# Moving the second half of an SBUF copy from ScalarE to VectorE in an attention and mixture-of-experts kernel

## Chip, cores and metric

The kernel runs on one core of one Trainium2 chip. The metric is the device time of one execution in microseconds (us); lower is better.

## What is computed

Three stages follow each other. First a chunked attention over 4 batches, 8 heads, 768 positions and a head size of 64: a chunk of 32 queries sees its own 32 keys, 16 to the left, 8 to the right and 8 memory keys. Then a soft mixture of experts, and then a top-2 mixture of experts, both over 3072 rows of 512 columns, with 8 experts of hidden size 1024. Cut to its core the reference is:

```python
for c in range(nc):                                   # 24 chunks of 32 queries
    k_full = concat([mem_k, k[:, :, l_start:r_end]])  # 8 + up to 56 keys
    v_full = concat([mem_v, v[:, :, l_start:r_end]])
    a = softmax(scale * q_c @ k_full.T)
    out[:, :, c_start:c_end] = a @ v_full
x = out.transpose(0, 2, 1, 3).reshape(3072, 512)
logits = x @ phi                                      # soft experts: 8 experts, 4 slots each
slot_input = softmax(logits, axis=0).T @ x
slot_out[e] = relu(slot_input[e] @ w1[e]) @ w2[e]
x = softmax(logits, axis=1) @ slot_out
top2 = the two largest of x @ w_gate + log1p(exp(x @ w_noise)) * noise
out[n] = sum over top2 of weight * (relu(x[n] @ w1[e]) @ w2[e])
```

## The kernel before

**Order of the work.** The program is written in the order in which each engine executes it (a manual schedule). Each engine runs its own instructions in that order and waits only for the semaphores that its next instruction needs. All large transfers are issued by SyncE in one queue; the small loads of `mem_v` are issued by GpSimd.

**The attention stage** (function `attention`, about the first 160 us) works through 32 items, numbered `i`. An item is one pair of heads of one batch and one half of the sequence (12 chunks); a pair of items shares one `q` and one `k` load. One pass of the main loop (a round here) makes these steps, each on the engine named:

- `qk(i+1)`: TensorE multiplies queries and keys into a PSUM tile `st` (lines 1062 and 1069).
- `mxr(i+1)` and `sub(i+1)`: VectorE clears the corner of `st`, takes the row maximum and subtracts it into `a` (lines 1077 to 1088).
- `tr(i+3)`: TensorE transposes a raw `q` or `k` tile, ScalarE copies it out of PSUM in four pieces (lines 1043 and 1050), and SyncE loads the raw tile three further on (line 996).
- `spread(i+1, 0)` and `spread(i+1, 1)`: copies of `v`, below.
- `expo(i+1)`: ScalarE takes the exponential (line 1092).
- `at(i)`, `atc(i)`: TensorE transposes the probabilities, ScalarE copies them out of PSUM into `aT` (lines 1097 and 1103).
- `av(i-1)`, `nrm(i-1)`: TensorE multiplies with `v` (line 1112), VectorE divides by the row sum into `xs` (lines 1121 to 1124). Behind them SyncE and GpSimd load the `v` of item `i+3` into the buffer that `av(i-1)` has just read (`load_v`, lines 1013 and 1022).
- `xt(i-2)`, `xtc(i-2)`: TensorE transposes `xs`, VectorE copies it into `xT` (lines 1135 and 1142). Six times in the stage `lg`, `lgc`, `lt` and `ltc` turn `xT` into logits (ScalarE line 1156, VectorE line 1166).
- In every second round SyncE issues a piece of 512 KB of the weights of the soft experts (`load_piece`, line 148).

The last four rounds are not in the loop; their steps stand in the table `ORDER`, mixed with the first softmax of the soft experts.

**The copies of `v`.** Four tiles `VB` in rotation hold the `v` of an item. Rows 0 to 63 belong to the first head of the pair and rows 64 to 127 to the second. Head `h` is loaded by one transfer of SyncE (28 rows of each chunk) and one of GpSimd (4 rows of `mem_v`). A loaded row holds two positions next to each other (128 columns), and one half of them has to stand on 32 other partitions for the product. `spread(i, h)` makes that copy, 32 partitions by 12 chunks by 64 columns, float32, SBUF to SBUF. It waits for the two transfers of its head, and `av(i)` waits for it:

```python
    def spread(i, h):
        ...
        if h:
            nc.scalar.activation(o, x, AF.Copy)       # second head: ScalarE, line 1031
        else:
            nc.vector.tensor_copy(o, x)               # first head: VectorE, line 1033
```

In the loop `spread(n, 0)` stands ahead of `sub(n)`, and `spread(n, 1)` behind `atc(i)` and ahead of `av(i-1)` and `nrm(i-1)`.

**After the attention.** From about 150 us on SyncE issues the weights of the remaining soft experts (line 148: into the arena that held `v`, `k` and the raw tiles, into `xs` and into two weight tiles), and then those of the first expert of the top-2 stage (line 200). TensorE computes the soft experts as the weights land (function `soft`, lines 238 to 258). The top-2 stage begins with its gate at about 230 us and ends with the kernel.

Of the kernel before, what the change touches and what calls it, by code (L numbers as in the profile page):

```python
# [13 lines left out]
AF = mybir.ActivationFunctionType  # L14
# [949 lines left out]
def attention(tc, nc, q, k, v, mem_k, mem_v, phi, xs, L, K, phis, arena, ab, wk, ps, load_piece):  # L964
# [35 lines left out]
    def vcols(i, p, n, col, cols, c0=0, c1=NH):  # L1000
        return custom(VB[i % NV][p:p + n], c0 * VC + col, [[VC, c1 - c0], [1, cols]])
# [25 lines left out]
    def spread(i, h):  # L1027
        o, x = (vcols(i, 32, 32, 64, D), vcols(i, 0, 32, 0, D)) if h == 0 else \
            (vcols(i, 96, 32, 130, D), vcols(i, 64, 32, VC, D))
        if h:  # L1030
            nc.scalar.activation(o, x, AF.Copy)  # L1031
        else:
            nc.vector.tensor_copy(o, x)  # L1033

    def tr(n):
        u, x = divmod(n, 2)
# [258 lines left out]
    nc.gpsimd.memset(one, 1.0)  # L1295
    load_v(3)
    spread(0, 0)
    spread(0, 1)
    qk(0)
    mxr(0)  # L1300
# [4 lines left out]
    for i in range(I0):  # L1305
# [5 lines left out]
        if i == 6:  # L1311
            nc.gpsimd.dma_start(phis, phi.rearrange("(j p) s -> p j s", p=128))
        spread(n, 0)
        sub(n)
        expo(n)
# [51 lines left out]
```

## Time and profile before

| | |
|---|---|
| median of 3 runs | 600.06 us (598.2 to 609.83) |
| the profiled execution: its time | 601.2 us |
| its span, first to last instruction | 599.4 us |
| mean granted clock of TensorE | 0.936 of full speed |
| busy: TensorE (PE) | 498.9 us, 83% |
| busy: VectorE (DVE) | 332.0 us, 55% |
| busy: ScalarE (ACT) | 291.6 us, 49% |
| busy: GpSimd (POOL) | 290.3 us, 48% |
| moved by DMA | 127.35 MB, mean 212 GB/s |

PE, DVE, ACT, POOL and SP are TensorE, VectorE, ScalarE, GpSimd and SyncE; PEld is TensorE's weight load, and SPq is SyncE issuing a transfer. L1033 is line 1033 of the kernel. A row names the line, the engine, the operation and the tiles as out<-in with partitions x elements, then xcount. "Idle before" is the idle time of the engine just ahead of the instruction, and the arrow says what ended it. The DMA share is the mean busy share of the 16 DMA engines; overlapping packets can carry it a little over 1.

### The profile page before, as it was taken

The page shows a single profiled execution, that of the slowest core. Times are in us where ns is not written, and L with a number is a line of the kernel's source. Part 1 is how long each engine was busy: PE and PEld are TensorE (multiplying, and loading weights), DVE is VectorE, ACT ScalarE, POOL GpSimd, SP SyncE. Part 2 cuts the span into 40 slices and gives each one's busy share as a digit, 9 for nine tenths or more (in the row PEclk, how much of TensorE's full clock was granted, in tenths as well). Part 3 has the DMA queues.
Part 4 walks back from the last instruction along what each step waited for, and adds up shares of the span by engine and source line. Part 5 has one row for each costly group of instructions (what it writes and reads, how often), then busy time and mean ns, then how long its engine had stood idle before and what let it go on. Part 6 is the DMA issues. An engine that isn't in the chain of part 4 may idle for free.

```text
span 599.4 us, 15297 instructions
## 1 busy us (share of the span) xinstructions
PE 498.9 (83%) x5437; PEld 274.1 (46%) x5437; DVE 332.0 (55%) x827; ACT 291.6 (49%) x510; POOL 290.3 (48%) x260
## 2 busy tenths in 40 slices
PE   5776988869889677365989899999999999989960
PEld 4655766647543124232534445545545455435520
DVE  6565767657863004898565755748566465622200
ACT  5876989868521104753532715526354263533210
POOL 6132322222012000693566765758576577877662
PEclk9998999999999867597989989999999999989995
DMA  9999999999999998959388696887869876436552
GB/s 206 231 217 213 241 240 262 229 221 241 315 412 362 412 415 241 349 179 254 52 248 226 111 265 152 233 226 170 224 150 264 215 183 119 80 69 111 75 63 26
DMA packets 99509, 127.35 MB, mean 212 GB/s; under 512 B 19238, under 2 KB 68026, under 8 KB 99434
## 3 DMA queue, kind: packets, MB, share of 16 engines
q1 hardware_dynamic: 79866, 109.30, 60.7%
q0 software_dynamic: 19152, 16.89, 21.2%
q8 instruction: 49, 0.80, 0.6%
q14 instruction: 26, 0.21, 0.1%
q10 hardware_dynamic: 416, 0.15, 0.1%
HBM read 94.84 MB, written 20.42 MB: 192 GB/s over the span
## 4 chain that ended last, share of the span: by engine, by line
PE 37%; DVE 7%; DMA 5%; issue 4%; POOL 3%; ACT 2%; SPq 0%; POOLq 0%; DVEq 0%; ACTq 0%
PE l L739 30%; DMA out_dram<-y,idx 4%; PE l L705 3%; POOL out_dram L770 2%; PE g L362 2%; DVE W L428 1%; DMA C<-G 1%; DVE W L544 1%; PE l L736 1%; DVE lo L715 1%; POOL cg L664 1%; ACT W L424 1%; DVE G L411 1%; DVE W L812 1%; ACT hi L707 0%
## 5 line engine op out<-in xcount | busy, mean ns | idle before, releaser
L770 POOL DMA_INDIRECT out_dram<-y,idx x96 | 155.8, 1622 | 83.3 <-DMA out_dram<-y,idx 40.7
L739 PE MATMUL l<-W,hi 128*128 (+1 forms) x768 | 182.5, 392 | 1.2 <-DVE W L428 0.8
L715 DVE SCALAR_TENSOR_TENSOR lo<-l,hi 128x1024 f16<-128x1024 f32 x49 | 59.9, 1222 | 112.3 <-ACT hi L707 97.8
L739 PEld LDWEIGHTS <-hi 128*128 128x128 f16 x768 | 75.2, 100 | 88.9 <-issue 14.3
L757 ACT ACTIVATE y<-l,gw 128x512 f32<-128x512 f32 x49 | 33.5, 684 | 156.1 <-PE l L739 94.0
L739 PE MATMUL l<-W,lo 128*128 (+1 forms) x384 | 90.8, 379 | 4.6 <-DVE lo L715 4.6
L1022 POOL DMA_DIRECT2D arena<-in_mem_v_dram x64 | 39.3, 615 | 105.1 <-PE av L1112 105.1
L664 POOL DMA_INDIRECT cg<-table,idx x49 | 51.1, 1044 | 20.4 <-issue 10.5
L739 PEld LDWEIGHTS <-lo 128*128 128x128 f16 x384 | 36.9, 98 | 48.5 <-DVE lo L715 5.2
L707 ACT ACTIVATE hi<-l 128x1024 f16<-128x1024 f32 x49 | 50.2, 1024 | 10.3 <-PE l L705 10.2
L1069 PE MATMUL st<-arena,qT 128*32 128x112 f32 (+2 forms) x768 | 31.8, 271 | 16.2 <-ACT arena L1050 9.9
L428 DVE SCALAR_TENSOR_TENSOR W<-w,sc,W 128x1024 f16<-128x1024 f32 x31 | 42.3, 1390 | 0.2
L1050 ACT ACTIVATE qT<-tr 64x384 f32<-64x384 f32 x64 | 33.2, 518 | 9.3 <-PE tr L1043 8.2
L1033 DVE COPY arena<-arena 32x768 f32<-32x768 f32 x32 | 17.8, 556 | 35.2 <-DMA arena<-in_v_dram 30.6
L1043 PE MATMUL tr<-cf,arena 128*128 128x128 f32 x192 | 31.2, 304 | 6.2 <-DMA arena<-in_q_dram 5.4
L424 ACT ACTIVATE W<-w,sc 128x1024 f16<-128x1024 f32 x32 | 35.7, 1149 | 0.2
L1112 PE MATMUL av<-arena,aT 128*32 128x130 f32 x768 | 29.3, 283 | 4.2 <-issue 3.5
L1050 ACT ACTIVATE arena<-tr 64x384 f32<-64x384 f32 x64 | 30.9, 484 | 2.3 <-PE tr L1043 1.6
L374 DVE TENSOR_REDUCE mxp<-w 128x1 f32<-128x2048 f32 x13 | 29.6, 2275 | 0.0
L1043 PEld LDWEIGHTS tr<-cf,arena 128*128 128x128 f32 x192 | 22.9, 153 | 13.8 <-issue 6.7
L1062 PE MATMUL st<-arena,qT 128*32 128x16 f32 x768 | 25.7, 188 | 2.8 <-issue 2.8
L1031 ACT ACTIVATE arena<-arena 32x768 f32<-32x768 f32 x32 | 26.9, 842 | 1.6 <-issue 0.7
(268 smaller groups left out, 680.3 us busy)
## 6 DMA issues: line engine op xcount, KB each, us to landing
w<-in_moe_w_dram SPq DMA_DIRECT2D x88, 512.0 KB
arena<-in_moe_w_dram SPq DMA_DIRECT2D x28, 512.0 KB
arena<-in_v_dram SPq DMA_DIRECT2D x62, 168.0 KB
arena<-in_q_dram SPq DMA_DIRECT2D x16, 384.0 KB
arena<-in_k_dram SPq DMA_DIRECT2D x16, 384.0 KB
xs<-in_moe_w_dram SPq DMA_DIRECT2D x12, 512.0 KB
out_dram<-zt SPq DMA_DIRECT2D x14, 384.0 KB
C<-G SPq DMA_DIRECT2D x21, 256.0 KB
```

What stands on the lines that cost most here:

```text
L424: nc.scalar.activation(hi, w2, AF.Copy, scale=sc[:, rk, 5:6])
L428: stt(lo, w2, sc[:, rk, 5:6], hi, op0=OP.mult, op1=OP.subtract)
L664: nc.gpsimd.indirect_dma_start(out=CG[i], out_offset=None, in_=table, in_offset=bass.IndirectOffsetOnAxis(ap=idx[:, i:i + 1], axis=0))
L707: nc.scalar.activation(HI[i], p, AF.Relu)
L715: stt(LO[i].rearrange("p k t -> p (k t)"), p.rearrange("p k t -> p (k t)"), 0.0, HI[i].rearrange("p k t -> p (k t)"), op0=OP.max, op1=OP.s ...
L739: nc.tensor.matmul(P2[i], h[i][:, k, :], dyn(W2f, i, w * 4096 + 512 * k, 512, RG.get(i)), start=x == 0 and k == 0, stop=x == last and k == 7)
L757: nc.scalar.activation(YV[i], P2.pop(i), AF.Copy, scale=GW.pop(i))
L770: nc.gpsimd.indirect_dma_start(out=o, out_offset=bass.IndirectOffsetOnAxis(ap=idx[:, i:i + 1], axis=0), in_=y[:, DH * h:DH * h + DH], in_o ...
L1022: nc.gpsimd.dma_start(vcols(i, p + 28, 4, col, 128), bass.AP(tensor=mem_v.tensor, offset=mem_v.offset + (b * H + 2 * hp + h) * NMEM * D, a ...
L1043: nc.tensor.transpose(p[:, T, :], src[:, h, T, :], identf)
L1050: nc.scalar.activation(o, i, AF.Copy)
L1069: nc.tensor.matmul(st[32 * j:32 * j + 32, g, :, w0:w1], QT[u][:, 32 * c:32 * c + 32], kb[:, :, 16 * c + w0:16 * c + w1], start=True, stop= ...
```

## The change

Both halves of the copy are made by VectorE; nothing else is edited.

```diff
     def spread(i, h):
         o, x = (vcols(i, 32, 32, 64, D), vcols(i, 0, 32, 0, D)) if h == 0 else \
             (vcols(i, 96, 32, 130, D), vcols(i, 64, 32, VC, D))
-        if h:
-            nc.scalar.activation(o, x, AF.Copy)
-        else:
-            nc.vector.tensor_copy(o, x)
+        nc.vector.tensor_copy(o, x)
```

The lines behind it stand three lines higher in the changed kernel: 1050 is 1047 there, 1033 is 1030, and so on. Names as `xT_89` and `xT_90` are the two tiles `xT`.

ScalarE, one round of the loop and the start of the next, before:

```order
L1050 ACTIVATE arena<-tr 64x384 x4
L1092 ACTIVATE a<-a 128x384
L1103 ACTIVATE aT<-at 128x384
L1031 ACTIVATE arena<-arena 32x12x64
L1050 ACTIVATE qT<-tr 64x384 x4
```

and with the change:

```order
L1047 ACTIVATE arena<-tr 64x384 x4
L1089 ACTIVATE a<-a 128x384
L1100 ACTIVATE aT<-at 128x384
L1047 ACTIVATE qT<-tr 64x384 x4
L1089 ACTIVATE a<-a 128x384
```

The copy `arena<-arena` is gone, and the four copies of the next transpose (`<-tr`) follow `aT<-at` at once.

VectorE, one round of the loop, before:

```order
L1079 MEMSET st 32x4x4
L1082 TENSOR_REDUCE mx<-st 128x6
L1033 COPY arena<-arena 32x12x64
L1088 TENSOR_TENSOR a<-st,mx 128x384
L1121 TENSOR_SCALAR rc<-av 128x6
L1122 RECIPROCAL rc<-rc 128x6
L1124 TENSOR_TENSOR xs<-av,rc 128x3x128
L1142 COPY xT_89<-xt 128x384
```

and with the change:

```order
L1076 MEMSET st 32x4x4
L1079 TENSOR_REDUCE mx<-st 128x6
L1030 COPY arena<-arena 32x12x64
L1085 TENSOR_TENSOR a<-st,mx 128x384
L1030 COPY arena<-arena 32x12x64
L1118 TENSOR_SCALAR rc<-av 128x6
L1119 RECIPROCAL rc<-rc 128x6
L1121 TENSOR_TENSOR xs<-av,rc 128x3x128
L1139 COPY xT_89<-xt 128x384
```

The second copy stands behind the subtraction and ahead of the division of `nrm` and of the copy `xT<-xt`.

VectorE at the end of the attention, from the last row maximum on, before:

```order
L1082 TENSOR_REDUCE mx<-st 128x6
L1142 COPY xT_89<-xt 128x384
L1088 TENSOR_TENSOR a<-st,mx 128x384
L1033 COPY arena<-arena 32x12x64
L1121 TENSOR_SCALAR rc<-av 128x6
L1122 RECIPROCAL rc<-rc 128x6
L1124 TENSOR_TENSOR xs<-av,rc 128x3x128
L1142 COPY xT_90<-xt 128x384
```

and with the change:

```order
L1079 TENSOR_REDUCE mx<-st 128x6
L1139 COPY xT_89<-xt 128x384
L1030 COPY arena<-arena 32x12x64
L1085 TENSOR_TENSOR a<-st,mx 128x384
L1030 COPY arena<-arena 32x12x64
L1118 TENSOR_SCALAR rc<-av 128x6
L1119 RECIPROCAL rc<-rc 128x6
L1121 TENSOR_TENSOR xs<-av,rc 128x3x128
L1030 COPY arena<-arena 32x12x64
L1139 COPY xT_90<-xt 128x384
```

Two copies are added there: that of item 30 ahead of the last subtraction, and that of item 31 ahead of `xT_90<-xt`. The order on TensorE, GpSimd and SyncE is the same in both kernels.

## Rows read from the trace of the kernel before

**Rows 1.** Page, 40 slices of the span (15 us each): busy tenths, GB/s.
```profile
DVE  6565767657863004898565755748566465622200
ACT  5876989868521104753532715526354263533210
...
DMA  9999999999999998959388696887869876436552
GB/s 206 231 217 213 241 240 262 229 221 241 315 412 362 412 415 241 349 179 254 52 248 226 111 265 152 233 226 170 224 150 264 215 183 119 80 69 111 75 63 26
```

**Rows 2.** Busy time by stretch (us from the span's start).
```profile
core 0: us, PE busy (x) PEld busy (x) DVE busy (x) ACT busy (x) POOL busy (x), PEclk, DMA share, GB/s
...
15.00:150.00 135.00, 108.28 (x2418) 80.44 (x2416) 86.84 (x226) 111.05 (x204) 34.48 (x56) 0.97 1.05 233
150.00:176.00 26.00, 22.25 (x358) 12.99 (x356) 20.71 (x56) 10.37 (x20) 0.80 (x2) 1.00 1.05 356
176.00:232.00 56.00, 43.83 (x457) 17.33 (x456) 9.22 (x26) 6.49 (x12) 6.80 (x16) 0.86 1.04 396
...
60.00:76.00 16.00, 15.20 (x357) 11.36 (x356) 12.78 (x33) 15.47 (x30) 4.72 (x8) 1.00 1.02 238
```

**Rows 3.** Groups by line, 0 to 160 us: busy us, mean ns, idle before.
```profile
L1022 POOL DMA_DIRECT2D arena<-in_mem_v_dram x64 | 39.3, 615 | 105.1 <-PE av L1112 105.1
...
L1031 ACT ACTIVATE arena<-arena 32x768 f32<-32x768 f32 x31 | 26.1, 842 | 0.8
...
L1033 DVE COPY arena<-arena 32x768 f32<-32x768 f32 x32 | 17.8, 556 | 35.2 <-DMA arena<-in_v_dram 30.6 <-issue 3.0 <-DMA arena<-in_mem_v_dram 1.3
...
L1142 DVE COPY xT<-xt 128x384 f32<-128x384 f32 x27 | 14.8, 548 | 0.2
```

**Rows 4.** Waits, 0 to 160 us: total us, times, longest.
```profile
DVE arena L1033 <- DMA arena<-in_v_dram: 30.6, 22, 2.8
```

**Rows 5.** Timeline of ACT, one round: start us, us, instruction.
```profile
82.65 1.97 ACT L1050 ACTIVATE arena<-tr 64x384 f32<-64x384 f32 x4
84.65 0.53 ACT L1092 ACTIVATE a<-a 128x384 f32<-128x384 f32 x1
85.20 0.49 ACT L1103 ACTIVATE aT<-at 128x384 f32<-128x384 f32 x1
85.71 0.84 ACT L1031 ACTIVATE arena<-arena 32x768 f32<-32x768 f32 x1
86.58 2.14 ACT L1050 ACTIVATE qT<-tr 64x384 f32<-64x384 f32 x4
```

**Rows 6.** Timeline of DVE, one round from copy to copy.
```profile
88.10 0.55 DVE L1033 COPY arena<-arena 32x768 f32<-32x768 f32 x1 [1.63 <-DMA arena<-in_v_dram]
88.69 0.56 DVE L1088 TENSOR_TENSOR a<-st,mx 128x384 f32<-128x384 f32 x1
89.16 0.15 DVE L1121 TENSOR_SCALAR rc<-av 128x6 f32<-128x6 f32 x1
...
90.78 0.56 DVE L1082 TENSOR_REDUCE mx<-st 128x6 f32<-128x384 f32 x1
92.03 0.55 DVE L1033 COPY arena<-arena 32x768 f32<-32x768 f32 x1 [0.69 <-DMA arena<-in_v_dram]
```

**Rows 7.** Timeline around 40 to 53 us: a load of v, and the copies.
```profile
39.72 1.18 SPq L1013 DMA_DIRECT2D arena<-in_v_dram  x2
40.19 0.55 DVE L1033 COPY arena<-arena 32x768 f32<-32x768 f32 x1 [2.54 <-DMA arena<-in_v_dram]
...
44.13 1.55 POOL L1022 DMA_DIRECT2D arena<-in_mem_v_dram  x2 [3.80 <-PE av L1112]
...
44.41 0.55 DVE L1033 COPY arena<-arena 32x768 f32<-32x768 f32 x1 [0.99 <-DMA arena<-in_v_dram]
...
48.48 1.18 POOL L1022 DMA_DIRECT2D arena<-in_mem_v_dram  x2 [2.80 <-PE av L1112]
...
50.44 0.55 DVE L1033 COPY arena<-arena 32x768 f32<-32x768 f32 x1 [2.80 <-DMA arena<-in_v_dram]
...
52.68 0.84 ACT L1031 ACTIVATE arena<-arena 32x768 f32<-32x768 f32 x1
```

**Rows 8.** SyncE's waits, 151 to 235 us: total us, times, longest.
```profile
SPq L148 <- DMA arena<-in_moe_w_dram: 15.8, 19, 0.9
SPq L148 <- DMA xs<-in_moe_w_dram: 12.6, 11, 2.4
```

**Rows 9.** Timeline behind the attention: the slots' inputs, then waits of PE.
```profile
176.09 0.23 DVE L1258 COPY phis<-sm 128x64 f32<-128x64 f32 x1 [0.32 <-PE sm L1255]
...
206.27 2.24 PE L238 MATMUL p<-arena,phis 128*32 128x256 f32 x16 [4.03 <-DMA arena<-in_moe_w_dram]
...
216.40 2.24 PE L238 MATMUL p<-arena,phis 128*32 128x256 f32 x16 [2.82 <-DMA arena<-in_moe_w_dram]
...
226.48 0.60 ACT L300 ACTIVATE so<-po 128x512 f32<-128x512 f32 x1 [4.79 <-PE po L258]
```

## Prediction

> **What bounds the kernel now.** I read the slices of the page first, then the busy times by stretch, the groups of the attention stage, and last the timelines of single rounds.
>
> The slices show DMA at nine tenths or more from the first slice to the fifteenth, that is to about 225 us, while neither VectorE nor ScalarE is full there for long [rows 1]. By stretch, the DMA share is 1.05 in 15 to 150 us at 233 GB/s, 1.05 in 150 to 176 at 356 and 1.04 in 176 to 232 at 396 [rows 2]. The transfers are a stream without a hole, all of it fixed by the program, and the top-2 stage begins only when the soft experts are through: TensorE waits for their weights at 206.27 and 216.40, and their sum is copied out at 226.48 [rows 9]. The change touches nothing behind 162 us or so, hence the question is whether it makes this stream longer, or lets it end sooner.
>
> In the attention the share of 1.05 alone proves little: it is also 1.02 in 60 to 76 us, where ScalarE is busy for 15.47 of 16 us and so sets the pace itself [rows 2]. What tells the two kinds of rounds apart is the wait ahead of VectorE's copy: 30.6 us in total for `in_v`, at 22 of the 32 copies [rows 3, 4]. I call these rounds DMA-paced and the other ten engine-paced. In the stretch of 135 us there are 29 rounds, 4.66 us each. A load of v issued in one round is used two copies later: the one issued at 39.72 is copied at 50.44, after a last wait of 2.80 [rows 7]. So a load needs some 10 us from issue to use, two rounds' worth of other transfers lying ahead of it in the queue. That queue does not run dry if VectorE is half a microsecond late.
>
> **The change part by part.**
>
> *Off ScalarE.* A round of ScalarE without a wait is 86.58 - 82.65 = 3.93 us, and the copy takes 86.58 - 85.71 = 0.87 of it with its gap [rows 5]. All 32 go: 32 x 0.87 = 27.8 us less work on ScalarE, and its round falls to 3.06.
>
> *Onto VectorE.* The group of the first head's copy has the same shape and type, 556 ns, against ScalarE's 842 [rows 3]; with its gap it is 88.69 - 88.10 = 0.59 [rows 6]. That is 32 x 0.59 = 18.9 us more on VectorE. A round of VectorE, without its waits, is from the copy at 88.10 to the one at 92.03 less the wait of 0.69: 92.03 - 88.10 = 3.93, and 3.93 - 0.69 = 3.24 [rows 6]. It becomes 3.24 + 0.59 = 3.83. Against 3.93 of ScalarE now, the bound of an engine-paced round moves from ScalarE to VectorE and falls by 0.10; ten such rounds give -1.0 us. What is late next is VectorE itself.
>
> *The copy's price, from both sides.* The nearest row is the first head's 556 ns. From below I have no reason for less than that. From above: a copy out of PSUM of 384 elements takes 548 ns [rows 3], so at that rate 768 elements would take up to 2 x 548 = 1096 ns. The round would then be 3.24 + 1.13 = 4.37, 0.44 over ScalarE's, and ten rounds would cost +4.4. I take 0.59, since the row is of the same operation.
>
> *The added wait.* VectorE now waits for the second head's load too, with `nrm`, the copy to `xT` and the next row maximum queued behind it; `av` waits for `nrm` and SyncE's next load of v for `av`. ScalarE never shows this wait, 0.8 us in all [rows 3], because its copy comes late: at 52.68, 2.24 after VectorE's at 50.44 [rows 7]. On VectorE the second copy may start 0.59 + 0.47 to 0.6, about 1.1 to 1.2, after the first. The wait lies between 0 and 2.24 - 1.1 = 1.1 us a round. The second load of 168 KB follows the first in the queue; at 233 GB/s that is 0.72 us, less than 1.1. I take 0, and keep for the range a round in four at 0.5: 8 x 0.5 = +4.
>
> *DMA-paced rounds.* There the first copy's wait averages 30.6 / 22 = 1.4 us [rows 4]. The added 0.59 comes behind that wait and eats into the next one. The landings do not move: 0.
>
> *GpSimd.* Its issue of two `mem_v` loads takes 1.55 us at 44.13, when a copy of VectorE (44.41) falls into it, and 1.18 at 48.48, where none does [rows 7]: 0.37 more. At most one issue pair a round meets one more copy, 32 x 0.37 = 11.8 us on an engine that idles 105.1 us there [rows 3]. The Trainium skill (SBUF — State Buffer, the section on its two separate sides) says that a float32 copy within SBUF on VectorE takes the port pair that GpSimd needs to write its descriptors, so that such a load starts only behind the copy; the two issues agree with it. By that rule the sum could rise, by the rows it stays as it is, since SyncE's load and not `mem_v` ends 30.6 of the 31.9 us of DMA waits [rows 3].
>
> *The end of the attention.* Up to three more copies, 3 x 0.59 = 1.8 us, stand on VectorE behind 150 us, where it is busy 20.71 of 26 us [rows 2]. The inputs of the soft experts are ready at 176.09; TensorE then works off the weights that have landed, and waits 4.03 us for the next at 206.27, and 2.82 at 216.40 [rows 9]. The 1.8 us vanish in the 4.03. SyncE's issues there wait for earlier weights to land, 19 and 11 times [rows 8], so that the stream does not start later either.
>
> *The sum.* Against the profiled execution's own 601.2 us (span 599.4, 1.8 around it): engine-paced rounds -1.0, DMA-paced 0, added wait 0, end 0. The -1.0 ends in a stream that is full until 232 us, and I count none of it: 601.2. The profiled execution is 1.1 over the median of the three runs, so the median becomes about 600.0. About 2% is what a measurement of this kernel can tell from no change.
>
> **The rivals.**
>
> *VectorE becomes the pace of every round.* If the waits for v are not a full queue but the travelling time of loads that are issued late, then each delay of `nrm`, and with it of `av` and of the next load, is added to the round. The price is 32 x 0.59 = 18.9 us: 600.0 + 18.9 = 618.9, slower by 3.1%. For it: the rate of 233 GB/s in the attention is far below the 396 behind it at the same share [rows 2], so the share does not prove that the transfers could go no faster. Against it: a load has 10 us between issue and use, and `av` would have to be the last thing that it waits for. It decides once the wait ahead of the first copy is gone in most rounds, that is when the mean of 1.4 us is eaten. Chance 0.06.
>
> *ScalarE's relief comes through.* ScalarE is the fullest engine of 15 to 150 us, 111.05 of 135 [rows 2]. If earlier transposes let `q`, `k` and v be loaded earlier and the transfers keep up, 0.87 a round is won, 31 x 0.87 = 27 us: 573.0, faster by 4.5%. Against it: VectorE's 3.83 stands in the way in just those rounds that ScalarE sets. Chance 0.03.
>
> *GpSimd's loads become the last to land.* With 11.8 us, all of it on the path, 611.8, slower by 2.0%, on the edge; with half of it 606. Against it: GpSimd's idle time of 105.1 us. Chance 0.04, half of it over 2%.
>
> *The copy is not made at the first head's rate:* +4.4, 604.4. Chance 0.07, within 2%.
>
> **How the numbers follow.** The forecast of 600.0 has 0.80, the copy at a slower rate 0.07, VectorE as the pace 0.06, GpSimd 0.04, ScalarE's relief 0.03. Faster by over 2%: 0.03. Slower by over 2%: 0.06 + 0.02 = 0.08. Within 2%: 0.89. Low end: the -1.0 counted in full from the lowest run of before, 598.2 - 1.0, is 597.2, and I go to 596.5. High end: the added waits at +4 or the slower copy at +4.4 give 604 to 604.4, and I go to 605. That holds the forecast and the slower copy, 0.87, less the scatter of the runs.
>
> **What would show it.** Right: VectorE has 64 copies `arena<-arena` of about 0.56 us; ScalarE's busy time in the attention falls by 27 us and its idle time grows as much; the wait for `in_v` ahead of VectorE's copies shrinks by up to 19 us in total; the DMA share stays above 1 until about 230 us; the first wait of TensorE for the arena's weights still stands near 206 us, up to 2 us shorter. Wrong in the direction of slower: the waits for v vanish, the last rows of the attention end some 10 to 20 us later, and the stream has holes. Wrong in the direction of faster: rounds of 3.8 us throughout, a rate over 260 GB/s in the attention, and the last soft weights landed well ahead of 225 us.

## The result and the profile after

The changed kernel takes 603.52 us in the median (600.61 to 611.41, 19 runs), the kernel before 602.55 us (593.46 to 609.83, 19 runs). The ratio is 1.0059 with an interval of 1.0034 to 1.0085: no change by the 2% that count here, but off 1. Such a ratio leaves out runs that lie over 1.5% above the fastest of their own kernel, and as the fastest run of before, 593.46 us, stands alone, that is eleven of its 19 runs and two of the other's. The medians are nearer to each other (603.52 / 602.55 = 1.0016), and over all 19 runs each the means are 604.28 and 603.31 us, a difference of 1.0 plus or minus 2.4.

The profiled execution takes 602.78 us with a span of 600.9, against 601.2 and 599.4. The slices of the page, which answer to [rows 1]:

```profile
DVE  6676978776874102899385554766647475442200
ACT  4754856565421202673252532726345272543310
...
DMA  9999999999999999967479597787988876446552
GB/s 198 235 222 208 238 215 259 217 206 242 268 411 361 412 411 326 316 219 184 110 165 279 75 254 219 207 199 167 240 199 234 221 146 169 78 85 113 75 62 28
```

VectorE is fuller in most of the first ten slices and ScalarE emptier, and DMA stays at nine tenths. The full stretch ends in the seventeenth slice instead of the fifteenth. The busy times by stretch, as [rows 2]:

```profile
15.00:150.00 135.00, 107.49 (x2334) 79.69 (x2334) 100.77 (x247) 84.58 (x172) 33.04 (x53) 0.95 1.05 227
150.00:176.00 26.00, 20.94 (x371) 13.19 (x366) 21.77 (x52) 8.71 (x18) 2.36 (x4) 0.93 1.06 326
176.00:232.00 56.00, 45.34 (x497) 17.66 (x489) 13.10 (x38) 7.86 (x16) 6.82 (x16) 0.91 1.04 398
...
60.00:76.00 16.00, 16.00 (x366) 12.34 (x367) 14.52 (x36) 13.26 (x27) 5.13 (x8) 1.00 1.03 231
```

In 15 to 150 us ScalarE is 26.5 us less busy (111.05 to 84.58) and VectorE 13.9 us more (86.84 to 100.77). DMA has the same share of 1.05 at 227 GB/s instead of 233. The groups of the attention stage (0 to 160 us), as [rows 3], and its waits, as [rows 4]:

```profile
L1022 POOL DMA_DIRECT2D arena<-in_mem_v_dram x64 | 39.4, 617 | 110.0 <-PE av L1109 109.9
L1030 DVE COPY arena<-arena 32x768 f32<-32x768 f32 x61 | 33.8, 554 | 25.5 <-DMA arena<-in_v_dram 19.5 <-DMA arena<-in_mem_v_dram 2.8 <-issue 1.9
```

```profile
ACT a L1089 <- DVE a L1085: 32.5, 23, 3.4
DVE arena L1030 <- DMA arena<-in_v_dram: 19.5, 17, 2.2
```

The copy lasts 554 ns, as long as the first head's did. VectorE waits 19.5 us for v, at 17 copies, where it waited 30.6 us at 22. ScalarE has become the engine that waits: 32.5 us for VectorE's subtraction, where it waited 16.1 before. The timeline of VectorE in two rounds without a wait (start us, us, instruction), where [rows 6] showed one of before:

```profile
64.13 0.56 DVE L1079 TENSOR_REDUCE mx<-st 128x6 f32<-128x384 f32 x1
64.72 0.55 DVE L1030 COPY arena<-arena 32x768 f32<-32x768 f32 x1
65.30 0.56 DVE L1085 TENSOR_TENSOR a<-st,mx 128x384 f32<-128x384 f32 x1
65.89 0.55 DVE L1030 COPY arena<-arena 32x768 f32<-32x768 f32 x1
66.48 0.17 DVE L1118 TENSOR_SCALAR rc<-av 128x6 f32<-128x6 f32 x1
...
67.38 0.55 DVE L1163 TENSOR_REDUCE L<-xt 128x96 f32<-128x384 f32 x1
67.84 0.55 DVE L1139 COPY xT<-xt 128x384 f32<-128x384 f32 x1
...
68.58 0.56 DVE L1079 TENSOR_REDUCE mx<-st 128x6 f32<-128x384 f32 x1
...
83.31 0.56 DVE L1079 TENSOR_REDUCE mx<-st 128x6 f32<-128x384 f32 x1
...
87.28 0.56 DVE L1079 TENSOR_REDUCE mx<-st 128x6 f32<-128x384 f32 x1
```

From row maximum to row maximum a round takes 87.28 - 83.31 = 3.97 us, and one with the reduction of the logits (L1163) in it 68.58 - 64.13 = 4.45. At the first round VectorE's second copy meets a wait of its own:

```profile
11.34 0.55 DVE L1030 COPY arena<-arena 32x768 f32<-32x768 f32 x1 [1.92 <-issue]
13.14 0.55 DVE L1030 COPY arena<-arena 32x768 f32<-32x768 f32 x1 [1.25 <-DMA arena<-in_mem_v_dram]
13.76 0.09 DVE L1074 MEMSET st<- 32x32 f32 x1
13.88 0.56 DVE L1079 TENSOR_REDUCE mx<-st 128x6 f32<-128x384 f32 x1
```

Last, the waits behind the attention, as [rows 9] (timelines of PE and ACT):

```profile
209.99 0.81 PE L238 MATMUL p<-arena,phis 128*32 128x256 f32 x8 [2.06 <-DMA arena<-in_moe_w_dram]
...
220.12 0.70 PE L238 MATMUL p<-arena,phis 128*32 128x256 f32 x8 [4.08 <-DMA arena<-in_moe_w_dram]
```

```profile
230.63 0.60 ACT L300 ACTIVATE so<-po 128x512 f32<-128x512 f32 x1 [5.22 <-PE po L258]
```

The first of these waits is 2 us shorter, but it and the end of the soft experts (`so`, 230.63 against 226.48) come 4 us later. By that one pair of profiles the change costs 4 us up to there; more profiles follow below.

### The profile page after: what moved, and what is told of

The parts are those of the page before. It is cut to its first block, busy times and chain, and to the rows that moved or that the text cites. A ratio compares the mean times of both kernels' runs of the same rounds, so it can differ in the third digit from the quotient of the medians.

```text
span 600.9 us, 15288 instructions
## 1 busy us (share of the span) xinstructions
PE 501.2 (83%) x5437; PEld 276.6 (46%) x5437; DVE 352.1 (59%) x859; ACT 263.3 (44%) x478; POOL 291.2 (48%) x260
## 4 chain that ended last, share of the span: by engine, by line
PE 39%; DVE 5%; DMA 5%; issue 3%; ACT 2%; POOL 2%; SPq 0%; POOLq 0%; DVEq 0%; ACTq 0%
PE l L739 32%; DMA out_dram<-y,idx 4%; PE l L705 3%; PE g L362 2%; POOL out_dram L770 2%; DMA C<-G 1%; PE l L736 1%; DVE lo L715 1%; ACT hi L707 1%; ACT W L424 1%; DVE G L411 1%; DVE W L812 1%; DVE W L428 0%; DVE W L544 0%; PE ct L669 0%
## 5 line engine op out<-in xcount | busy, mean ns | idle before, releaser
L739 PE MATMUL l<-W,hi 128*128 (+1 forms) x768 | 179.8, 388 | 0.4 <-issue 0.4
L739 PE MATMUL l<-W,lo 128*128 (+1 forms) x384 | 92.5, 385 | 4.0 <-DVE lo L715 4.0
L664 POOL DMA_INDIRECT cg<-table,idx x49 | 53.3, 1089 | 20.2 <-issue 11.3
L1030 DVE COPY arena<-arena 32x768 f32<-32x768 f32 x64 | 35.4, 554 | 25.6 <-DMA arena<-in_v_dram 19.5
L1109 PE MATMUL av<-arena,aT 128*32 128x130 f32 x768 | 32.0, 300 | 6.1 <-issue 4.3
L1089 ACT ACTIVATE a<-a 128x384 f32<-128x384 f32 x32 | 16.7, 523 | 34.7 <-DVE a L1085 34.4
```

The costliest lines, as they stand in the source:

```text
L664: nc.gpsimd.indirect_dma_start(out=CG[i], out_offset=None, in_=table, in_offset=bass.IndirectOffsetOnAxis(ap=idx[:, i:i + 1], axis=0))
L739: nc.tensor.matmul(P2[i], h[i][:, k, :], dyn(W2f, i, w * 4096 + 512 * k, 512, RG.get(i)), start=x == 0 and k == 0, stop=x == last and k == 7)
```

## The experiments

Two questions were open. Are the 0.6% of the first comparison the kernel's, and are the 18.9 us added to VectorE covered by its waits for the transfers? The theory is that they are covered, as long as a round of VectorE without waits stays below the kernel's mean round of 4.66 us. One rival is that VectorE's time counts in every round, another that it counts only at the start and the end of the attention, where nothing covers it, and a third that the copies disturb GpSimd's loads.

Each kernel was timed beside runs of the kernel before on the same chip. In the profiles I compare five marks, in us: the first and the last row maximum of the attention, the issue of the first weight piece into the arena, the slots' inputs (`phis`), and the copy of the soft experts' sum (`so`, L300).

**Both kernels again, three times.** `c_before`, `c_before_2`, `c_before_3` and `c_after`, `c_after_2`, `c_after_3` are the two kernels with no edit, each pair on another chip.

> The kernel before once more, unchanged, to see how far the marks of one execution scatter. Marks: the start of the last attention item's row maximum (157.2 us in the first profile), the first issue of a soft weight into the arena (151.6) and the landing of the stream, seen as the end of TensorE's last soft product (226.4). If scatter made the difference between the two first profiles, these marks lie 2 us or more away from those; by both theories that blame the change they lie within 1 us.

> The changed kernel once more, unchanged. Marks of its first profile: last row maximum 163.7, first arena weight 156.2, and the soft experts about 3.7 later than before. Theory A (VectorE is the pace of the rounds that hardly wait for v) and theory B (the copy itself slows the transfers or GpSimd) both expect these within 1 us and 1.0059 +- 0.004 in time; scatter would bring them back towards the marks of before.

> The kernel before a third time, for the scatter. Marks so far: last row maximum 157.2 and 160.4, soft experts' sum copied out at 226.5 and 227.5. Theory C (the transfers cover VectorE) expects 226 to 229 and a mean time within 0.3% of the reference runs.

> The changed kernel a third time. Marks so far: soft experts' sum at 230.6 and 226.9. Theory C: anywhere from 226 to 231, mean time within 0.3% of the kernel before on the same chip. Theory A (the change costs 0.6%): near 230.5 again, and a mean 3 us or more over the kernel before.

> The kernel before a fourth time, on the same chip as the next. Marks of the soft experts' sum so far 226.5, 227.5, 226.1: 226 to 228 again if the difference to the changed kernel is more than scatter.

> The changed kernel a fourth time. Marks so far 230.6, 226.9, 230.5. A price of 2 to 4 us expects 229 to 231 and a mean time 2 to 4 us over the kernel before on this chip; no price expects a mean within 1 us.

Against the kernel before, the changed one has 0.9978 (0.9936 to 1.0020), 0.9950 (0.9868 to 1.0032) and 1.0010 (0.9961 to 1.0059). The kernel before against itself has 0.9998 (0.9960 to 1.0036), 1.0015 (0.9969 to 1.0061) and 0.9894 (0.9781 to 1.0007). The 1.0059 did not come again. Over all runs of the first comparison and of these three, the changed kernel has a mean of 603.56 us in 55 runs (standard error 0.46) and the kernel before 603.70 in 144 (0.29): a difference of -0.1, plus or minus 1.1 us. The marks of these profiles, and of those versions further down that keep the transfers as they are:

| | first max | last max | arena weight | `phis` | `so` |
|---|---|---|---|---|---|
| before | 13.17 | 157.19 | 151.63 | 176.09 | 226.48 |
| c_before | 13.27 | 160.42 | 154.17 | 178.80 | 227.49 |
| c_before_2 | 14.73 | 158.07 | 152.29 | 176.51 | 226.12 |
| c_before_3 | 13.64 | 160.19 | 154.66 | 178.80 | 229.00 |
| after | 13.88 | 163.71 | 156.19 | 183.20 | 230.63 |
| c_after | 13.88 | 160.31 | 154.18 | 179.80 | 226.90 |
| c_after_2 | 13.98 | 163.57 | 156.79 | 183.07 | 230.50 |
| c_after_3 | 13.73 | 161.51 | 154.80 | 181.00 | 229.31 |
| m_memset | 14.44 | 161.48 | 155.21 | 181.30 | 228.72 |
| d_double | 14.15 | 165.96 | 158.10 | 186.39 | 231.26 |
| d_triple | 15.51 | 168.80 | 161.17 | 191.65 | 232.64 |
| e_ends | 13.31 | 162.66 | 157.57 | 182.18 | 232.29 |
| e_late | 13.73 | 158.92 | 151.72 | 178.40 | 226.39 |

The same program moves by some 3 us from profile to profile, so one pair of profiles proves nothing of this size: `c_before` and `c_after` end their attention 0.1 us apart. But four profiles of each kernel do show a delay. The last row maximum comes at 159.0 in the mean before and at 162.3 after, 3.3 us later. `phis` comes 4.2 us later, 177.6 against 181.8, and there the two sets do not overlap; the latest of the kernel before (here `c_before`) and the earliest of the changed one (`c_after`):

```profile
178.80 0.23 DVE L1258 COPY phis<-sm 128x64 f32<-128x64 f32 x1 [0.32 <-PE sm L1255]
```

```profile
179.80 0.23 DVE L1255 COPY phis<-sm 128x64 f32<-128x64 f32 x1 [0.31 <-PE sm L1252]
```

At `so` 2.1 us are left (227.3 and 229.3), the sets overlap, and the times do not show them. So some 3 to 4 of the 18.9 us are not covered within the attention; what is left of them behind it is not seen in the times.

**More work on VectorE, in and out of the copy.** `m_memset` leaves the copy on ScalarE, and lets VectorE clear columns that nothing reads, for about the copy's time. `d_double` and `d_triple` add one and two more copies to the changed kernel, into such columns.

```diff
# m_memset: the kernel before with
+    scr = carve(768)
...
             nc.scalar.activation(o, x, AF.Copy)
+            nc.vector.memset(scr[96:128, 0:610], 0.0)
# d_double: the changed kernel with (d_triple: for the rows 96 and 64)
+    scr = carve(768)
...
         nc.vector.tensor_copy(o, x)
+        if h:
+            nc.vector.tensor_copy(custom(scr[96:128], 0, [[D, NH], [1, D]]), x)
```

> The kernel before, with a memset of 32x610 (some 0.56 us) added on VectorE where the second copy stands in the changed kernel; ScalarE keeps its copy. It reads nothing and waits for no load. Theory A: VectorE's time is the same as with the change and ScalarE is not relieved, so the first arena weight is issued 3 to 6 us later than before and the time is 1.005 to 1.012. Theory B: no added copy of v, so marks within 1 us of before and 1.000 +- 0.003.

> The changed kernel with a third copy a round on VectorE: the second head's block once more, into unused space. A round of VectorE without waits is then 3.97 + 0.59 = 4.56 us, 5.0 with the logits' reduction, against a mean of 4.66 before. Theory A: most rounds lose their wait, the first arena weight is issued 6 to 14 us later than in the changed kernel, time 1.015 to 1.03 against before. Theory B: the cost is one more of the same, some 3.5 us, time 1.010 to 1.013. If the transfers alone set the pace: within 1 us of the changed kernel.

> The changed kernel with two more copies a round on VectorE, the pieces of weights between the loads as before. By the round without cover (3.98 with one added copy, 4.44 with two, so 4.90 with three, 5.38 in the rounds with the logits' reduction) VectorE's round now exceeds the mean round of 4.66 of the kernel before. Theory C: the cover is used up, VectorE is the pace, last row maximum near 14 + 25 x 4.90 + 6 x 5.38 = 169 us, soft experts' sum at 234 to 238, time 1.010 to 1.018 against before. If the transfers set the pace whatever VectorE does: as with one added copy, within 0.4%.

`m_memset` has 1.0066 (1.0019 to 1.0113, median 606.04) and `so` at 228.72, inside the scatter of the table. That would be as much as the first comparison gave for the whole change, but the next run, with more work on VectorE, has less; by itself it decides nothing. Its `phis` at 181.30 lies among those of the changed kernel, though no copy of v was added; by this one profile the delay comes with another instruction of that length in that place as well, and needs nothing that a copy does to GpSimd.

`d_double` has 0.9965 (0.9913 to 1.0018, median 604.76, against 604.31 of the runs of before beside it). By the means of all runs it takes 0.4 us more than `c_after` on the same chip, plus or minus 3.0. A third copy in each round, 32 more in all, adds nothing that the time shows; the rival by which VectorE's time counts in full in every round falls. In the marks it isn't free: the attention ends 3.7 us later than the mean of the changed kernel, and `so` is 1.9 later.

```profile
165.96 0.56 DVE L1082 TENSOR_REDUCE mx<-st 128x6 f32<-128x384 f32 x1
```

What pays for most of it is the wait for v (15 to 150 us), in the kernel before, the changed one and `d_double`:

```profile
DVE arena L1033 <- DMA arena<-in_v_dram: 30.1, 21, 2.8
```

```profile
DVE arena L1030 <- DMA arena<-in_v_dram: 18.9, 16, 2.2
```

```profile
DVE arena L1031 <- DMA arena<-in_v_dram: 7.2, 10, 1.8
```

With the fourth copy it is gone. The timeline of VectorE in `d_triple`, two row maxima on end, and the last one of the attention:

```profile
87.19 0.56 DVE L1083 TENSOR_REDUCE mx<-st 128x6 f32<-128x384 f32 x1
...
92.20 0.56 DVE L1083 TENSOR_REDUCE mx<-st 128x6 f32<-128x384 f32 x1
...
168.80 0.56 DVE L1083 TENSOR_REDUCE mx<-st 128x6 f32<-128x384 f32 x1
```

Its round is 92.20 - 87.19 = 5.01 us, more than the mean round of 4.66, and no wait for v is left in its list. The attention ends at 168.80, near the 169 that was expected, and the ratio is 1.0126 (1.0039 to 1.0212, from six runs; median 609.14 beside 604.14): with the fourth copy the kernel is about 5 us longer, with the third it isn't. That fits a cover that ends where the round without waits passes the mean round. The marks show no such step, though. From no added copy to three the attention ends at 159.0, 162.3, 166.0 and 168.8, some 3 us later with each, and `so` stands at 232.64, only 1.4 us behind `d_double`'s and below the 234 to 238 expected. So where the 5 us arise is not shown.

**The cover taken away.** In the `l_` kernels the 16 pieces of weights that are loaded during the attention (512 KB each) are issued behind it, so that the transfers of the attention are about a quarter lighter (16 x 512 KB = 8.4 MB, of 233 GB/s x 145 us = 34 MB):

```diff
             attention(tc, nc, q, k, v, ...)
+            for i in range(16):
+                load_piece(i)
...
-        if s == 0:
-            load_piece(i // 2)
```

The pieces 14 and 15 are also taken out of `ORDER`. `l_before`, `l_after` and `l_double` are the kernel before, the changed one and `d_double` with this; `l_bal` is `x_bal`, below, with it.

> The kernel before, with the 16 pieces of soft weights (and the two writes of zeros that go with them) issued behind the attention's loads instead of between them; the work is the same. If transfers cover VectorE in the attention (theory C), the waits for v now vanish and ScalarE is the pace: rounds of 3.93 us, 4.3 with a logits copy, last row maximum near 137 to 140 us against 157 to 160. If v, q and k alone fill the transfers (theory D), the waits stay and it comes near 150.

> The changed kernel with the same pieces moved behind the attention. Theory C: VectorE is the pace, rounds of 3.97 us and 4.44 with the logits' reduction, as the changed kernel's rounds without a wait have; last row maximum 1 to 4 us later than with ScalarE's copy. Theory D: within 1 us of it.

> Three copies a round on VectorE and the pieces moved behind the attention. Theory C: rounds of 4.56 and 5.03 us, last row maximum 17 to 21 us later than with ScalarE's copy and the time 2 to 3.5% over that of the same arrangement before, since nothing covers the third copy now. Theory D: 0 to 5 us.

> Both copies of v on VectorE, but the copy of xT out of PSUM (VectorE 548 ns) moved to ScalarE, with the pieces behind the attention. Theory C: VectorE's round falls to about 3.45 us and ScalarE's is 3.06 + 0.5 = 3.6, so rounds of 3.6 to 3.7 and a last row maximum 8 to 12 us earlier than the arrangement before. Theory D: no gain, within 2 us of it.

The last row maximum in `l_before`, `l_after` and `l_double`:

```profile
140.02 0.56 DVE L1084 TENSOR_REDUCE mx<-st 128x6 f32<-128x384 f32 x1
```

```profile
140.93 0.56 DVE L1081 TENSOR_REDUCE mx<-st 128x6 f32<-128x384 f32 x1
```

```profile
152.57 0.56 DVE L1084 TENSOR_REDUCE mx<-st 128x6 f32<-128x384 f32 x1
```

Without the weights the attention ends some 17 to 20 us sooner (157.2 to 160.4 before), so the transfers did set its length. With them away ScalarE as the pace and VectorE as the pace come out 0.91 us apart: this is the change's own price where nothing covers it, by one profile each. The rounds have almost no part in it. The 11th and the 30th row maximum of `l_before` and of `l_after`:

```profile
53.38 0.56 DVE L1084 TENSOR_REDUCE mx<-st 128x6 f32<-128x384 f32 x1
...
131.17 0.56 DVE L1084 TENSOR_REDUCE mx<-st 128x6 f32<-128x384 f32 x1
```

```profile
53.44 0.56 DVE L1081 TENSOR_REDUCE mx<-st 128x6 f32<-128x384 f32 x1
...
131.33 0.56 DVE L1081 TENSOR_REDUCE mx<-st 128x6 f32<-128x384 f32 x1
```

These 19 rounds take 77.79 us in the one and 77.89 in the other; 0.75 of the 0.91 us come from the two rounds behind them. A third copy then costs 152.57 - 140.93 = 11.6 us, where under the weights it moved the same mark by 3.7. Against `l_before` it is 12.55 us, where 17 to 21 were expected. The time goes with it: `l_before` 0.9935 (0.9858 to 1.0012), `l_after` 0.9983 (0.9926 to 1.0041), `l_double` 1.0151 (1.0057 to 1.0245, from four runs). By the means of all runs `l_double` takes 8.5 us more than `l_after`, plus or minus 4.2, against the 0.4 plus or minus 3.0 with the weights in the stream. Rounds of VectorE in `l_after`, two row maxima, and what stands between them at the second copy:

```profile
82.20 0.56 DVE L1081 TENSOR_REDUCE mx<-st 128x6 f32<-128x384 f32 x1
...
83.38 0.56 DVE L1087 TENSOR_TENSOR a<-st,mx 128x384 f32<-128x384 f32 x1
83.97 0.55 DVE L1032 COPY arena<-arena 32x768 f32<-32x768 f32 x1
84.55 0.16 DVE L1120 TENSOR_SCALAR rc<-av 128x6 f32<-128x6 f32 x1
...
86.18 0.56 DVE L1081 TENSOR_REDUCE mx<-st 128x6 f32<-128x384 f32 x1
```

The round is 3.98 us. Who sets it is seen in the busy times of 60 to 130 us (columns as in [rows 2]), of `l_before` and of `l_after`:

```profile
60.00:130.00 70.00, 63.29 (x1484) 47.41 (x1476) 55.92 (x142) 67.61 (x124) 20.23 (x35) 1.00 0.76 188
```

```profile
60.00:130.00 70.00, 66.01 (x1526) 48.31 (x1517) 64.91 (x159) 51.94 (x108) 21.56 (x35) 1.00 0.79 192
```

ScalarE is busy for 67.61 of 70 us in the one; in the other it has 51.94, and VectorE is at 64.91. TensorE (first column) is as full there, 66.01, but it is not the pace: with the same work on it rounds of 3.5 us occur in `l_bal`, and rounds grow to 4.44 when VectorE alone gets a third copy (`l_double`). But a shorter attention wins nothing: `so` comes at 228.61 in `l_before` and 228.92 in `l_after`, as late as with the weights in their place, which fits that the same bytes are then still to be moved. `l_bal` has many rounds of 3.5 us, but its wait for `mem_v` grows to 9.3 us (5.6 in `l_before`), its attention ends at 143.00, no sooner than `l_after`'s and not the 8 to 12 us sooner that were expected, and its ratio is 0.9951 (0.9889 to 1.0012).

**The start and the end.** `e_ends` gives the second copies of the items 0, 29, 30 and 31 back to ScalarE. `e_late` moves the second copy to the end of the round, behind the copy to `xT`. `x_bal` moves the copy to `xT` to ScalarE, to even out the two engines.

```diff
# e_ends
-        nc.vector.tensor_copy(o, x)
+        if h and i in (0, 29, 30, 31):
+            nc.scalar.activation(o, x, AF.Copy)
+        else:
+            nc.vector.tensor_copy(o, x)
# e_late
         atc(i)
-        spread(n, 1)
...
             xtc(i - 2)
+        spread(n, 1)
# x_bal
-        nc.vector.tensor_copy(XT[z][:, hp, :], p.rearrange("p t n -> p (t n)"))
+        nc.scalar.activation(XT[z][:, hp, :], p.rearrange("p t n -> p (t n)"), AF.Copy)
```

> The changed kernel with the second copies of items 0, 29, 30 and 31 back on ScalarE: the start and the end of the attention as before, the rest as changed. Both theories: the first row maximum returns from 13.9 to 13.2-13.3 us, and from the last row maximum to the slots' inputs it takes 18.4 to 18.9 us as before, where the changed kernel took 19.5. Theory C: no gain in time, within 0.3% of the changed kernel, as both ends are swallowed by waits. If the ends are the price: 1 to 2 us less.

> The changed kernel, with the second copy behind the copy of xT at the end of the round, so that the division of nrm and with it the next load of v do not stand behind it. VectorE's time is the same. If the rest of the price comes from what is queued behind the copy (nrm, av, the issue of the next load of v): mark of the soft experts' sum at 226 to 228. If VectorE's time as such is the price: 229 to 231.

> The changed kernel, with the copy of xT out of PSUM (548 ns) moved from VectorE to ScalarE; the pieces of weights stay between the loads. VectorE's round without a wait falls from 3.97 to some 3.45 us. Theory A' (what is left of the change's price, 2.6 us in the mark of the soft experts' sum, is VectorE's time): the mark returns to 226 to 228, as before the change. Theory B (the copy of v itself slows the transfers or GpSimd, since both copies are still VectorE's): it stays at 229 to 231. Time within 0.4% either way.

`e_ends` has 1.0002 (0.9943 to 1.0061). Its first row maximum stands at 13.31, within the 13.2 to 14.7 of the kernel before, but from the last maximum to `phis` it takes 182.18 - 162.66 = 19.5 us, as in the changed kernel (183.20 - 163.71) and not the 18.4 to 18.9 of the kernel before. The copies at the end are thus not what makes the end longer, and nothing is won by giving them back; what lengthens it stays open. Its `so` at 232.29 is later than any of the changed kernel's. `e_late` has 1.0034 (0.9988 to 1.0081), and no gain in the time, but its marks are as early as in the kernel before, with `phis` at 178.40, `so` at 226.39 and the last maximum here:

```profile
158.92 0.56 DVE L1079 TENSOR_REDUCE mx<-st 128x6 f32<-128x384 f32 x1
```

VectorE's time is the same in it, so by what was expected of this run the delay comes of what is queued behind the second copy (`nrm`, `av`, the next load of v) and not of VectorE's time in the round as a whole. It is one profile, and the program scatters by 3 us, so this isn't shown. `x_bal` has 1.0049 (1.0001 to 1.0097); its profiled execution was its longest (612.32 us), so its marks are not used (`so` at 235.00, outside both expectations), and why it gains nothing stays open. No version beat either kernel.

## Why the prediction was right or wrong

**The time.** 600.0 was forecast and 603.52 measured, within the range, and the forecast of no change holds by 2%. Most of the 3.5 us between them is no effect of the change: the 600.06 us that the forecast started from are the median of three runs, and the same kernel has 602.55 in 19. That 603.52 still lies within the range is luck in part. The first comparison put the ratio off 1 all the same, at 1.0059, on the side of slower where the terms pointed to faster or nothing. Three repeats did not show that again, and all runs together leave -0.1 plus or minus 1.1 us. Whether some tenths of a per cent remain can't be settled by these runs.

**What bounds the kernel: right in the main.** The transfers cover most of VectorE's added time. The same third copy moves the end of the attention by 11.6 us without the weights in the stream and by 3.7 with them, and the time by 8.5 plus or minus 4.2 against 0.4 plus or minus 3.0. For the change itself the cover matters less: in rounds that do not wait, VectorE's new pace is as long as ScalarE's old one. The rival in which VectorE becomes the pace of every round had its point right, "once the wait ahead of the first copy is gone in most rounds", but the change eats 11 of the 30.6 us only.

**The step that failed: "the bound of an engine-paced round moves from ScalarE to VectorE and falls by 0.10; ten such rounds give -1.0 us".** VectorE's round was to be 3.24 + 0.59 = 3.83; it is 3.97, so it does not fall. Where nothing covers the rounds, 19 of them take 77.89 us with the change and 77.79 without, and the last row maximum comes 0.91 us later, not 1.0 sooner (`l_after` against `l_before`). Both sides of the step were mis-sized, and rows of before could have told it:

- A copy that is put between two instructions costs more than its own 0.59. Before, the division's first instruction starts 89.16 - 88.69 = 0.47 after the subtraction [rows 6]. Now a copy stands behind the subtraction and starts 65.89 - 65.30 = 0.59 after it. So the insertion costs 0.59 + 0.12 = 0.71, and 3.24 + 0.71 = 3.95, which is the measured round but for 0.02.
- ScalarE's 3.93 is a round with the four copies of a `k` tile, 1.97 us. The next round's four, of a `q` tile, take 2.14 [rows 5]. Such a round is 3.93 + 0.17 = 4.10, and the two kinds alternate, so that ScalarE's mean round is 4.0.

One round was also taken for all on VectorE: six rounds hold the reduction of the logits, which adds 67.84 - 67.38 = 0.46, and they take 4.45. But ScalarE has an extra copy for the logits in these rounds too, so this does not tell the kernels apart.

**The terms put at 0 (DMA-paced rounds, added wait, end): too low inside the attention.** In four profiles of each kernel the last row maximum comes 3.3 us later and `phis` 4.2 us later. That is a part of the price of the rival whose chance was 0.06, by which a delay of `nrm`, `av` and the next load adds to the round: some 3 of its 18.9 us. `e_late` points that way, and the cause stays open.

**The copy's price: right.** 554 ns, against 556 taken and 1096 as the upper bound. ScalarE's busy time fell from 291.6 to 263.3 us, by 28.3 where 27.8 were forecast; VectorE's rose from 332.0 to 352.1, by 20.1 where 18.9 were.

**The added wait: small, but not 0 everywhere.** In the loop the second copy finds its load landed in all rounds but one, where it waits 0.56 us; at the end of the attention it waits twice more, 0.9 us together. In the first round it waits 1.25 us for `mem_v`. In the first pair of profiles the first row maximum comes 0.7 us later, but over four of each the means are 13.7 and 13.9, so a price of this wait isn't shown.

**DMA-paced rounds: the mechanism right, the 0 not.** The wait for v shrank by 30.6 - 19.5 = 11.1 us, within the 19 that were allowed for. That pays for little more than half of the 20.1 us added; the 3.3 us by which the attention ends later are part of the rest.

**GpSimd: right.** An issue of `mem_v` takes 617 ns in the mean, 615 before [rows 3], though twice the copies can meet it, and GpSimd idles 110.0 us there. Over four profiles each the mean is 599 to 615 ns before and 617 to 641 after, so 64 issues take about 1 us more. The rival falls: the wait for `mem_v` ahead of the copies is 2.8 us, nearly half of which is the first round's. The Trainium skill (SBUF — State Buffer, the section on its two separate sides) has such a load start only behind a copy of this kind. Single issues did last longer, 12 of 64 with up to 958 ns where before there were 8 with up to 962, the rest about 590; all but the first of these met a copy, but of the issues that met one 21 of 32 lasted no longer. On an engine that idles the rule has no price here.

**The end of the attention: half right.** From the last maximum to `phis` it grew from 18.4 to 18.9 us in the kernel before to 19.5 in all four profiles of the changed one. TensorE's first wait for the arena's weights shrank from 4.03 to 2.06 us, as forecast, though it ended at 209.99 and not near 206. In `c_after` it ends at 206.82, with the same program. Over four profiles each it shrank from 3.9 to 4.1 us to 2.1 to 3.3: this is how 1.4 of the 4.2 us at `phis` vanish ahead of `so`.

**ScalarE's relief: worth nothing, as forecast.** The rounds that ScalarE set are now set by VectorE. And even an attention that is 17 to 20 us shorter (`l_before`) brings the end of the soft experts no nearer.

## What to carry to other kernels

Price an instruction that is added to an engine by the wait that stands ahead of it. As long as the engine's round without waits stays under the mean round, most of it is covered: here 32 copies of 18.9 us in all moved the end of the attention by some 3 us and the time by nothing that the runs show. Where no wait is left, it costs its time in every round (0.47 us in `l_double`). Adding the same instruction twice and three times shows in two runs where the time begins to feel it. Take the round without waits from row maximum to row maximum over several rounds, with the gaps of the neighbours between which the new instruction falls. And where a comparison says half a per cent, repeat it with the unchanged kernel beside it before looking for the cause: here the repeats took the effect away.

## What the hardware showed that was not expected

- Two copies of 32 x 768 float32 within SBUF, one right behind the other on VectorE, start 0.48 us apart although each lasts 0.55; behind a subtraction out of PSUM the same copy starts 0.59 later. In `l_double`:

```profile
85.07 0.55 DVE L1033 COPY arena<-arena 32x768 f32<-32x768 f32 x1
85.55 0.55 DVE L1035 COPY arena<-arena 32x768 f32<-32x768 f32 x1
```

- A DMA share over 1 tells nothing of the rate. It is 1.05 at 227 and 233 GB/s in the attention and 1.04 at 398 behind it. With the weights moved away it fell to 0.76 to 0.79 at 188 to 192 GB/s, in rounds that the engines set (`l_before` and `l_after`, above).
- Taking 8 MB of weights out of the attention's transfers shortened it by some 17 to 20 us and the kernel by nothing that these runs can tell.
